# A sum of two tiles made by an adding transfer in place of GpSimd's tensor_tensor

## The chip, the cores and the metric

The kernel runs on one core of one Trainium2 chip. The core has five engines, each with its own instruction stream: TensorE (PE; its weight loads are listed apart as PEld), VectorE (DVE), ScalarE (ACT), GpSimd (POOL) and SyncE (SP). They meet only at semaphores. Sixteen DMA engines move data between the chip's memory (HBM) and the on-chip SBUF, and within SBUF. PSUM is the memory that PE writes its products to. The metric is the device time of one execution in microseconds (us); lower is better.

## What is computed

Two parts, cut to what matters. The first is a causal convolution over the sequence with a softmax of seven taps for each of eight heads. The second, on its output x, is two products with a rational function between them:

```
w = softmax(weight)                     # 8 heads x 7 taps
x[s] = sum over k of w[k] * x_padded[s + k]
h = x @ w_in                            # 32768 x 192, 192 x 2048
P = a0 + a1*h + a2*h^2 + a3*h^3
Q = 1 + |b0|*|h| + |b1|*h^2
out = (P / (Q + 1e-6)) @ w_out          # 2048 x 192
```

Everything is float32 on the outside; there are 32768 tokens.

## The kernel before

The tokens are taken in 64 chunks of 512. For each chunk PE makes the convolution (steps c, as small matmuls with a band of taps), then the first product in eight units of 2 x 128 rows of h (steps g1; a unit is a tile of 128 x 1024 float32 in PSUM, named hp), and, one chunk later, the second product (steps g2, tile op) from the eight results g. Between the products stand the elementwise steps of a unit, named by letters:

- hs (ACT, L334): copies h from PSUM to SBUF. p (POOL, L340) and u (POOL, L347) begin the cubic from that copy: t = (-a3*hs - a2)*hs. In unit 3 ACT (L328) and VectorE begin it from PSUM; in units 4 and 7 ACT (L328) does p.
- v (DVE, L351): goes on with the cubic, and is the last reader of h.
- A (ACT, L354): |b0 h|. B (ACT, L357): |b1| h^2.
- Q (POOL, L360): A + B, written over A.
- L (ACT, L363): the logarithm of A + B + 1 + 1e-6, written over B. Y (ACT, L366): exp(-L), the reciprocal, tile y in PSUM, of which there is one.
- m (DVE, L370): the cubic times y. e (DVE, L375): y times the denominator, which it reads from A. g (DVE, L379): a Newton step that refines the quotient; its tile g feeds PE.

So in one unit Q waits for A and B, L waits for Q, Y for L, m for Y, and e reads A as well.

The order of the steps on PE, ACT, DVE and POOL is written out by hand: START is the first two rounds, with the conversion of the weights from float64 among them (steps wi and wo; `L227`, `L233`, `L237`, `L245` on DVE, `L241` on POOL), PLAN is one round of the steady part, used 61 times, and END is the rest. Each engine takes its steps strictly in that order, so a step that waits holds up all that is behind it on its engine. The steps on which the prediction rests stand so in PLAN (after the point: how many chunks late):

```
c0a.0 L7.2 m6.2 u1.1 g12a.1 O1.2 A1.1 e6.2 g12b.1 B1.1 Q0.1 g6.2 g20a.1 hs2.1 c0b.0 v1.1 g20b.1 Y7.2
c0c.0 p2.1 L0.1 ...
```

SBUF tiles come from pools: t, A, B have four buffers each, hs three, g eleven. DMAs are issued by SyncE: the inputs, two loads of x per chunk (xs) and two stores of results per chunk (out). GpSimd issues none.

Of the kernel before, what the change touches and what calls it, by code (L numbers as in the profile page):

```python
# [16 lines left out]
ALU = mybir.AluOpType  # L17
# [20 lines left out]
F64_MIN = float(np.uint32(0x38000000).view(np.float32))  # L38


# The order in which the engines take the steps of one chunk of tokens: step, unit or half,
# piece; after the point, how many chunks later than the first step of its chunk it is taken.
PLAN = """
c0a.0 L7.2 m6.2 u1.1 g12a.1 O1.2 A1.1 e6.2 g12b.1 B1.1 Q0.1 g6.2 g20a.1 hs2.1 c0b.0 v1.1 g20b.1 Y7.2
c0c.0 p2.1 L0.1 m7.2 g13a.1 B2.1 u2.1 g13b.1 e7.2 A2.1 g20c.1 g7.2 A3.1 g20d.1 Q1.1 g21a.1 v2.1 Y0.1
# [6 lines left out]
g11a.0 m5.1 p0.0 B0.0 g11b.0 e5.1 u0.0 L6.1 g27a.1 g5.1 hs1.0 g27b.1 g27c.1 p1.0 v0.0 Y6.1 g27d.1  # L52
"""

# How a unit's cubic begins. H: on VectorE, from PSUM; U: on GpSimd; V: on ScalarE, then GpSimd.
MODES = "UUUHVUUV"

# The first two rounds, with the preparation of the weights (wi: w_in, wo: w_out; step, piece);
# after the point the chunk.
START = """  # L60
wia0.0 c0a.0 wim0.0 wis0.0 c1a.0 wid0.0 wia1.0 c1b.0 wio0.0 wim1.0 wir0.0 c1c.0 wis1.0 c0b.0 c0c.0
xh1.0 wid1.0 wia2.0 wih0.0 xl1.0 wio1.0 xh0.0 wir1.0 wim2.0 wid2.0 wia3.0 wil0.0 wia4.0 xl0.0 wis2.0
# [13 lines left out]
L6.0 e5.0 u0.1 wor7.0 hs1.1 g5.0 p1.1 Y6.0 v0.1 wor4.0  # L76
"""

# What remains after the last full round; after the point the chunks from the end.
END = """  # L80
u1.2 L7.3 m6.3 B1.2 O1.3 c0a.1 g12a.2 A1.2 g12b.2 Q0.2 e6.3 hs2.2 c0b.1 g6.3 Y7.3 g20a.2 v1.2 A2.2
B2.2 c0c.1 g20b.2 m7.3 g20c.2 p2.2 g20d.2 g21a.2 e7.3 g13a.2 g13b.2 g21b.2 g7.3 g21c.2 u2.2 xh0.1
# [26 lines left out]
def kernel(  # L109
# [12 lines left out]
    nc = tc.nc  # L122
# [13 lines left out]

    nc.scalar.preload_act_table_set("natural_log_exp_and_others")

# [1 line left out]
    wb_t = const.tile([P, NG, BW], F32, name="wb_t")  # L140
    mb_t = const.tile([P, NG, BW], F32, name="mb_t")
    wr_t = const.tile([P, NG, KT], F32, name="wr_t")
# [15 lines left out]
        nc.sync.dma_start(out=t[0:BLK, 0:3 * XF // 4], in_=xa[c])  # L158
        nc.sync.dma_start(out=t[BLK:, 3 * XF // 4:], in_=xb[c])

# [1 line left out]
    mx = const.tile([P, NG], F32, name="mx")  # L162
    sm = const.tile([P, NG], F32, name="sm")
    nc.vector.tensor_reduce(out=mx, in_=wr_t, axis=AX.X, op=ALU.max)
# [7 lines left out]
    nc.vector.tensor_tensor(out=wb_t, in0=wb_t, in1=mb_t, op=ALU.mult)  # L172
    nc.vector.tensor_tensor(out=wb_t, in0=wb_t, in1=sm[:, :, None].broadcast_to([P, NG, BW]), op=ALU.mult)

# [1 line left out]
    cf = const.tile([P, 6], F32, name="cf")  # L176
    nc.vector.tensor_scalar(cf[:, 0:4], ab_t[:, 0:4], -1.0, None, ALU.mult)
    nc.scalar.activation(out=cf[:, 4:6], in_=ab_t[:, 4:6], func=AF.Abs)
# [15 lines left out]
        scales.append(reg)  # L194
    r_be0, r_sq1, r_a3 = scales

# [1 line left out]
    # In integers: the upper word's digits, rebiased, then the lower word's, rounded, added.  # L198
    wh_t = const.tile([P, UPC, 2, 2, P], F32R, name="wh_t")
    wl_t = const.tile([P, UPC, 2, 2, P], F32R, name="wl_t")  # L200
    wo_t = const.tile([P, FT, D], F32, name="wo_t")
# [43 lines left out]
            nc.vector.tensor_tensor(out=wl_t[:, i].rearrange("p a b c -> p (a b c)"), in0=w["t"],  # L245
                                    in1=wh_t[:, i].rearrange("p a b c -> p (a b c)").bitcast(F32), op=ALU.subtract)

# [1 line left out]
    def stat(c, blk, g):  # L249
        t = xs_buf[c % 2].rearrange("p (m b g) -> p m b g", m=32, b=NBLK)  # L250
        return t[:, :, blk, g]
# [24 lines left out]
            xh = X[c, "B"]  # L276
            nc.vector.tensor_tensor(out=xh[64:P], in0=cps[0:64], in1=xh[0:64].bitcast(F32), op=ALU.subtract)

# [1 line left out]
    H = {}  # L280

    def gemm1(k, j):
# [5 lines left out]
        for n, (w, part, x) in enumerate(terms):  # L288
            nc.tensor.matmul(H[k][:, j, :], lhsT=w[:, i, part, j, :], rhs=x, start=(n == 0), stop=(n == len(terms) - 1))  # L289

# [1 line left out]
    G = {}  # L292
    O = {}

# [18 lines left out]
        nc.scalar.copy(out=ob, in_=O.pop((c, pair))[:, :, 0:D])  # L313
        nc.sync.dma_start(out=out_v[c, pair], in_=ob)

# [1 line left out]
    st = {}  # L317

    def flat(k):
# [37 lines left out]
        nc.scalar.activation(out=tile_of(k, "B", work), in_=flat(k), func=AF.Square, scale=r_sq1)  # L357

    def step_Q(k):
        nc.gpsimd.tensor_tensor(out=st[k]["A"], in0=st[k]["A"], in1=st[k]["B"], op=ALU.add)  # L360

    def step_L(k):
        nc.scalar.activation(out=st[k]["B"], in_=st[k]["A"], func=AF.Ln, bias=C_Q)  # L363
# [13 lines left out]
    def step_g(k):  # L377
# [1 line left out]
        nc.vector.scalar_tensor_tensor(out=g, in0=st[k]["y"], scalar=2.0, in1=g, op0=ALU.subtract, op1=ALU.mult)  # L379
        del st[k], H[k]  # L380

# [1 line left out]
    unit_steps = {"hs": step_hs, "p": step_p, "u": step_u, "v": step_v, "A": step_A, "B": step_B, "Q": step_Q,  # L383
                  "L": step_L, "Y": step_Y, "m": step_m, "e": step_e, "g": step_g}
    CP = {}
# [27 lines left out]
            else:  # L413
                unit_steps[kind](c * UPC + n)

# [1 line left out]
    def steps(text):  # L417
        return [(kind, int(n), "abcd".find(piece) if piece else 0, int(c))
                for kind, n, piece, c in re.findall(r"(g1|g2|w[io][a-z]|[A-Za-z]+)(\d)([a-d]?)\.(\d+)", text)]

    order = steps(START)
# [67 lines left out]
```

## Time and profile before

| | |
|---|---|
| median of 3 runs | 2808.53 us (2807.76 to 2809.02) |
| span of the profiled execution, first to last instruction | 2807.8 us |
| time of an execution beside that span | the three runs stand 0.0 to 1.2 us over the span; the median 0.7 us |
| busy share of the span | PE 98%, PEld 88%, DVE 96%, ACT 96%, POOL 96% |
| granted clock of PE, mean | 0.991 of full |
| DMA | 61.22 MB on SyncE's queue, 7.9% of 16 engines |

The profile is one execution, taken by the hardware profiler. Its page lists busy times, the chain of work that ended last, groups of instructions (line, engine, operation, tiles written <- read, shapes, count | busy us, mean ns of one | idle us just before them and what ended it), and DMA issues (size, median us from issue to landing). Other views of the same trace used here: the stages (a row for each stretch of time, with each engine's busy us and number of instructions), the waits (engine and line that waited, for whom, total us, times, longest), and the order of time (start us, duration us, instruction, and in brackets the idle time before it). A busy PE is not proof of PE at its peak, and idle time of an engine that does not set the pace costs nothing.

### The profile page before, as it was taken

What the parts mean: (1) busy time and instruction counts of PE and PEld (TensorE: products, weight loads), DVE (VectorE), ACT (ScalarE), POOL (GpSimd) and SP (SyncE); (2) the same over time, 40 slices, a digit from 0 to 9 for tenths busy, and PEclk for the clock granted to TensorE, in tenths of its full rate; (3) what the DMA queues carried; (4) which work ended last, traced back from release to release, by engine and by line L of the source; (5) the groups of instructions that cost most, each with busy time, mean ns of one, the idle gap of its engine ahead of it and who ended that gap; (6) DMA issues with size and microseconds to landing.
All of it is one profiled execution on the core that took longest, in us unless ns stands there. A gap on an engine that the chain in (4) does not pass through costs nothing.

```text
span 2807.8 us, 50193 instructions
## 1 busy us (share of the span) xinstructions
PE 2748.3 (98%) x20224; PEld 2458.2 (88%) x20224; DVE 2683.3 (96%) x2309; ACT 2688.4 (96%) x2990; POOL 2684.4 (96%) x1304
## 2 busy tenths in 40 slices
PE   4799999999999999999999999999999999999999
PEld 3688988988889889889889888888898898898888
DVE  8999999999999999999999999999999999999998
ACT  6899999999999999999999999999999999999997
POOL 6899999999999999999999999999999999999996
PEclk8899999999999999999999999999999999999999
DMA  4000000000000000000000000000000000000000
GB/s 136 10 16 25 22 16 25 22 16 25 21 17 22 19 22 22 19 22 22 16 25 22 16 25 22 16 22 19 22 22 19 22 22 16 25 22 16 25 9 15
DMA packets 49193, 64.43 MB, mean 23 GB/s; under 512 B 4672, under 2 KB 43840, under 8 KB 48960
## 3 DMA queue, kind: packets, MB, share of 16 engines
q1 hardware_dynamic: 48960, 61.22, 7.9%
q8 instruction: 159, 2.61, 0.4%
q14 instruction: 74, 0.61, 0.1%
HBM read 36.03 MB, written 25.17 MB: 22 GB/s over the span
## 4 chain that ended last, share of the span: by engine, by line
PE 96%; DVE 2%; issue 1%; ACT 0%; DMA 0%; SPq 0%; ACTq 0%; DVEq 0%
PE op L306 48%; PE hp L289 42%; PE cps L259 6%; DVE ad L227 0%; PE cps L306 0%; DVE t L351 0%; DVE wl_t L245 0%; DMA g<-in_w_in 0%; DVE g L370 0%; DVE y L375 0%; DVE tr L233 0%; DVE tr L237 0%; DVE wo_t L233 0%; DVE g L379 0%; DVE wo_t L237 0%
## 5 line engine op out<-in xcount | busy, mean ns | idle before, releaser
L306 PE MATMUL op<-wo_t,g 128*128 128x192 f32 x8128 | 1420.8, 326 | 0.0
L306 PEld LDWEIGHTS op<-wo_t,g 128*128 128x128 f32 x8128 | 1344.6, 189 | 43.9
L360 POOL TENSOR_TENSOR A<-A,B 128x1024 f32<-128x1024 f32 x512 | 1219.2, 2388 | 28.4 <-ACT B L357 26.1
L347 POOL TENSOR_TENSOR t<-t,hs 128x1024 f32<-128x1024 f32 x448 | 1077.9, 2406 | 48.6 <-ACT hs L334 16.3
L289 PE MATMUL hp<-xh,wh_t 128*128 128x512 f32 x2048 | 872.9, 426 | 45.9 <-DVE t L351 41.4
L370 DVE SCALAR_TENSOR_TENSOR g<-t,cf,y 128x1024 f32<-128x1024 f32 x512 | 654.4, 1278 | 57.0 <-ACT y L366 46.6
L351 DVE SCALAR_TENSOR_TENSOR t<-t,cf,hp 128x1024 f32<-128x1024 f32 x512 | 652.5, 1274 | 32.7 <-POOL t L347 29.9
L379 DVE SCALAR_TENSOR_TENSOR g<-y,g 128x1024 f32<-128x1024 f32 x512 | 626.9, 1224 | 17.5
L289 PE MATMUL hp<-xh,wl_t 128*128 128x512 f32 x2048 | 637.7, 393 | 0.0
L375 DVE SCALAR_TENSOR_TENSOR y<-A,y 128x1024 f32<-128x1024 f32 x512 | 625.5, 1222 | 0.0
L363 ACT ACTIVATE B<-A 128x1024 f32<-128x1024 f32 x512 | 547.0, 1069 | 0.2 <-POOL A L360 0.2
L366 ACT ACTIVATE y<-B 128x1024 f32<-128x1024 f32 x512 | 528.8, 1033 | 15.6 <-DVE g L379 14.6
L354 ACT ACTIVATE A<-hp 128x1024 f32<-128x1024 f32 x512 | 528.0, 1031 | 15.8 <-PE hp L289 15.7
L357 ACT ACTIVATE B<-hp 128x1024 f32<-128x1024 f32 x512 | 528.7, 1033 | 0.0
L289 PEld LDWEIGHTS hp<-xh,wh_t 128*128 128x128 f32 x2048 | 388.8, 190 | 124.4 <-DVE t L351 32.6
L334 ACT COPY hs<-hp 128x1024 f32<-128x1024 f32 x448 | 457.2, 1020 | 35.4 <-PE hp L289 34.1
L289 PEld LDWEIGHTS hp<-xh,wl_t 128*128 128x128 f32 x2048 | 388.2, 190 | 87.5
L289 PE MATMUL hp<-xl,wh_t 128*128 128x512 f32 x1024 | 405.5, 396 | 2.4 <-DVE xl L273 2.4
L340 POOL TENSOR_SCALAR t<-hs,cf 128x1024 f32<-128x1024 f32 x320 | 389.6, 1217 | 10.8 <-ACT hs L334 3.9
L328 ACT ACTIVATE t<-hp,cf 128x1024 f32<-128x1024 f32 x192 | 214.7, 1118 | 25.3 <-PE hp L289 22.8
L259 PEld LDWEIGHTS cps<-wb_t,xs 128*32 128x32 f32 x6876 | 162.5, 149 | 65.8 <-issue 64.3
L289 PEld LDWEIGHTS hp<-xl,wh_t 128*128 128x128 f32 x1024 | 195.4, 191 | 23.7 <-DVE xl L273 2.9
(49 smaller groups left out, 632.6 us busy)
## 6 DMA issues: line engine op xcount, KB each, us to landing
out<-ob SPq DMA_DIRECT2D x128, 192.0 KB, 2.0
xs<-in_xa SPq DMA_DIRECT2D x64, 324.0 KB, 3.9
xs<-in_xb SPq DMA_DIRECT2D x64, 108.0 KB, 3.7
g<-in_w_in SPq DMA_DIRECT2D x8, 512.0 KB, 9.4
g<-in_w_out SPq DMA_DIRECT2D x8, 384.0 KB, 9.3
wb_t<-in_wband SPq DMA_DIRECT2D x1, 174.0 KB, 2.4
mb_t<-in_mband SPq DMA_DIRECT2D x1, 174.0 KB, 2.4
wr_t<-in_wrep SPq DMA_DIRECT2D x1, 21.0 KB, 1.9
```

Of the source, the lines that this page charges most:

```text
L289: nc.tensor.matmul(H[k][:, j, :], lhsT=w[:, i, part, j, :], rhs=x, start=(n == 0), stop=(n == len(terms) - 1))
L306: nc.tensor.matmul(op[:, t, 0:D], lhsT=g[:, f % 2, tok:tok + P], rhs=wo_t[:, f, :], start=(f == 0 and t == 0), stop=(f == FT - 1 and t == 1))
L347: nc.gpsimd.tensor_tensor(out=t, in0=t, in1=st[k]["hs"], op=ALU.mult)
L351: nc.vector.scalar_tensor_tensor(out=t, in0=t, scalar=a1, in1=flat(k), op0=ALU.add, op1=ALU.mult)
L354: nc.scalar.activation(out=tile_of(k, "A", work), in_=flat(k), func=AF.Abs, scale=r_be0)
L357: nc.scalar.activation(out=tile_of(k, "B", work), in_=flat(k), func=AF.Square, scale=r_sq1)
L360: nc.gpsimd.tensor_tensor(out=st[k]["A"], in0=st[k]["A"], in1=st[k]["B"], op=ALU.add)
L363: nc.scalar.activation(out=st[k]["B"], in_=st[k]["A"], func=AF.Ln, bias=C_Q)
L366: nc.scalar.activation(out=tile_of(k, "y", ps_y), in_=st[k]["B"], func=AF.Exp, scale=-1.0)
L370: nc.vector.scalar_tensor_tensor(out=G[k].rearrange("p a b -> p (a b)"), in0=st[k]["t"], scalar=a0, in1=st[k]["y"], op0=ALU.add, op1=ALU.mult)
L375: nc.vector.scalar_tensor_tensor(out=y, in0=st[k]["A"], scalar=C_Q, in1=y, op0=ALU.add, op1=ALU.mult)
L379: nc.vector.scalar_tensor_tensor(out=g, in0=st[k]["y"], scalar=2.0, in1=g, op0=ALU.subtract, op1=ALU.mult)
```

## The change

The step Q is no longer an instruction of GpSimd that adds, but a transfer from SBUF to SBUF, issued by GpSimd at the same place in its order, which reads B and adds it to A where A lies. Comments of the file were blanked out as well, without moving a line.

```diff
     def step_Q(k):
-        nc.gpsimd.tensor_tensor(out=st[k]["A"], in0=st[k]["A"], in1=st[k]["B"], op=ALU.add)
+        nc.gpsimd.dma_start(out=st[k]["A"], in_=st[k]["B"], accum_op=ALU.add)
```

No step changes its place. On GpSimd, in the steady part, from Q of unit 7 to the three Q's that follow each other (units 1, 3, 2); before:

```order
L360 TENSOR_TENSOR A<-A,B 128x1024
L340 TENSOR_SCALAR t<-hs,cf 128x1024
L347 TENSOR_TENSOR t<-t,hs 128x1024
L340 TENSOR_SCALAR t<-hs,cf 128x1024
L347 TENSOR_TENSOR t<-t,hs 128x1024
L360 TENSOR_TENSOR A<-A,B 128x1024
L340 TENSOR_SCALAR t<-hs,cf 128x1024
L347 TENSOR_TENSOR t<-t,hs 128x1024
L360 TENSOR_TENSOR A<-A,B 128x1024 x3
```

and after (p and u of units 0 and 1 stand between the first two Q's, of units 7 and 0; p and u of unit 2 behind them):

```order
L360 DMA A<-B 128x1024
L340 TENSOR_SCALAR t<-hs,cf 128x1024
L347 TENSOR_TENSOR t<-t,hs 128x1024
L340 TENSOR_SCALAR t<-hs,cf 128x1024
L347 TENSOR_TENSOR t<-t,hs 128x1024
L360 DMA A<-B 128x1024
L340 TENSOR_SCALAR t<-hs,cf 128x1024
L347 TENSOR_TENSOR t<-t,hs 128x1024
L360 DMA A<-B 128x1024 x3
```

Only the kind of instruction is another. On ScalarE the order is the same too, but the semaphores differ. Around L of unit 7 (the first L363 here) and of unit 0 (the second), with what each instruction waits for, before:

```order
L363 ACTIVATE B<-A 128x1024 [waits Pool_49]
L313 COPY ob<-op 128x384 [waits DMAHW3_49,PE_49]
L354 ACTIVATE A<-hp 128x1024
L357 ACTIVATE B<-hp 128x1024
L334 COPY hs<-hp 128x1024 [waits PE_49]
L366 ACTIVATE y<-B 128x1024 [waits DVE_49,Activation_49]
L363 ACTIVATE B<-A 128x1024 [waits Pool_49]
```

and after:

```order
L363 ACTIVATE B<-A 128x1024 [waits DMASW7_49]
L313 COPY ob<-op 128x384 [waits DMAHW3_49,PE_49]
L354 ACTIVATE A<-hp 128x1024
L357 ACTIVATE B<-hp 128x1024
L334 COPY hs<-hp 128x1024 [waits PE_49,Pool_49]
L366 ACTIVATE y<-B 128x1024 [waits DVE_49,Activation_49]
L363 ACTIVATE B<-A 128x1024 [waits DMASW0_49]
```

L now waits for the transfer's landing (DMASW, one of eight semaphores in turn) and no longer for GpSimd's addition; the copy hs has a wait for GpSimd of its own, for a buffer that u has read, which L's wait covered before.

## The prediction, written before the result

> **What bounds the kernel now.** I read the page's busy times and chain first, then the table by stage, then who waits in the middle of the run, and last the order of time on ScalarE (ACT) and GpSimd (POOL) around one Q step. Page, then the stages (us, then busy us of PE, PEld, DVE, ACT and POOL with instructions, granted clock, DMA share, GB/s):
>
> ```profile
> PE 2748.3 (98%) x20224; PEld 2458.2 (88%) x20224; DVE 2683.3 (96%) x2309; ACT 2688.4 (96%) x2990; POOL 2684.4 (96%) x1304
> PE 96%; DVE 2%; issue 1%; ACT 0%; DMA 0%; SPq 0%; ACTq 0%; DVEq 0%
> ```
>
> ```profile
> 0.00:70.00 70.00, 31.71 (x283) 24.07 (x284) 61.70 (x71) 45.66 (x67) 48.36 (x33) 0.83 0.45 136
> 70.00:140.00 70.00, 52.45 (x328) 44.09 (x327) 67.66 (x63) 59.35 (x70) 62.65 (x33) 0.83 0.04 10
> 700.00:2100.00 1400.00, 1400.00 (x10362) 1254.62 (x10362) 1346.47 (x1149) 1364.94 (x1510) 1361.85 (x656) 1.00 0.08 21
> ```
>
> PE is busy in all 1400 us of the middle at the full clock, and the chain runs through PE: nothing that GpSimd gives up can shorten a round there. All of PE's idle time that could be had back lies in the first 140 us (38.3 + 17.6 us) and a few us at the end. But the others are close behind. A round (one chunk of tokens, eight units) takes 42.67 us, by the chain in order of time, where the same matmuls come back (start us, us):
>
> ```profile
> 1395.04 3.90 PE op L306 x24
> 1437.71 3.90 PE op L306 x24
> ```
>
> The 1400 us hold 32.8 rounds. Idle per round is then (1400 - 1364.94) / 32.8 = 1.07 us on ScalarE, 1.63 us on VectorE, 1.16 us on GpSimd. Who waits there (total us, times, longest):
>
> ```profile
> DVE g L370 <- ACT y L366: 21.1, 66, 0.5
> DVE t L351 <- POOL t L347: 15.5, 65, 0.4
> ACT hs L334 <- PE hp L289: 13.7, 33, 0.4
> ```
>
> No L step (L363, the logarithm) waits for Q, and PE waits for nobody. So the question is not what GpSimd saves but whether Q's result still comes in time for L, on a ScalarE that can lose 1.07 us in a round and no more.
>
> **What is taken off GpSimd.** From the page:
>
> ```profile
> L360 POOL TENSOR_TENSOR A<-A,B 128x1024 f32<-128x1024 f32 x512 | 1219.2, 2388 | 28.4 <-ACT B L357 26.1
> L347 POOL TENSOR_TENSOR t<-t,hs 128x1024 f32<-128x1024 f32 x448 | 1077.9, 2406 | 48.6 <-ACT hs L334 16.3
> ```
>
> 512 additions of 2.39 us, 1219 us, go; what it takes to issue a transfer comes in their place. Per round 8 x 2.38 = 19.0 us of 41.5 go, so an issue may cost up to 2.39 + 1.16 / 8 = 2.5 us before GpSimd becomes the bound. Worth in the middle: nothing, since PE has no wait to give back. VectorE's waits for u (15.5 us) become fewer, which PE doesn't feel.
>
> **What is added: Q becomes a transfer that ScalarE waits for.** Every transfer has 128 rows of 4 KB, 0.52 MB; B is read, A is read, A is written. What matters is the time from Q's turn on GpSimd to the semaphore on which L waits. I call it the landing, with the issue in it. What is allowed is read at unit 0, where Q and L stand closest. ScalarE (start us, us):
>
> ```profile
> 1377.58 1.02 ACT L357 ACTIVATE B<-hp 128x1024 f32<-128x1024 f32 x1
> 1379.57 1.01 ACT L334 COPY hs<-hp 128x1024 f32<-128x1024 f32 x1
> 1380.56 1.03 ACT L366 ACTIVATE y<-B 128x1024 f32<-128x1024 f32 x1
> 1381.52 1.04 ACT L363 ACTIVATE B<-A 128x1024 f32<-128x1024 f32 x1
> 1382.47 0.46 ACT L313 COPY ob<-op 128x384 f32<-128x384 f32 x1
> 1382.83 1.03 ACT L354 ACTIVATE A<-hp 128x1024 f32<-128x1024 f32 x1
> 1383.75 1.02 ACT L357 ACTIVATE B<-hp 128x1024 f32<-128x1024 f32 x1
> 1385.19 1.02 ACT L334 COPY hs<-hp 128x1024 f32<-128x1024 f32 x1 [0.42 <-PE hp L289]
> 1386.10 1.03 ACT L366 ACTIVATE y<-B 128x1024 f32<-128x1024 f32 x1
> 1387.06 1.05 ACT L363 ACTIVATE B<-A 128x1024 f32<-128x1024 f32 x1
> ```
>
> GpSimd beside it:
>
> ```profile
> 1380.69 1.20 POOL L340 TENSOR_SCALAR t<-hs,cf 128x1024 f32<-128x1024 f32 x1
> 1381.97 2.42 POOL L347 TENSOR_TENSOR t<-t,hs 128x1024 f32<-128x1024 f32 x1
> 1384.34 2.40 POOL L360 TENSOR_TENSOR A<-A,B 128x1024 f32<-128x1024 f32 x1
> ```
>
> B of unit 0 is ready at 1378.6 (first row), yet Q starts at 1384.34: in GpSimd's order it stands behind p and u of unit 1, and p begins when hs of unit 1 ends (1379.57 + 1.01). A less loaded GpSimd doesn't help: hs, p and u keep their times, so Q's turn stays where it is. L of unit 0 is the last row of ScalarE, at 1387.06. The gap is 2.72 us, just more than the 2.40 us of the addition. Behind a late L stand B and A of unit 2, A of unit 3, Y of unit 0 and all the rest of ScalarE; m on VectorE waits for that Y, and already waits for a Y twice in a round; POOL's next Q waits for a B behind it. Since hs, p, u and Q are all counted from a step of ScalarE ahead of L, the gap moves with ScalarE and the stall comes back every round. ScalarE takes up 1.07 us. So **a landing over 2.72 + 1.07 = 3.79 us makes every round longer by what it is over**, in each of the 61 rounds of the table PLAN.
>
> The others have more room: unit 1's Q began at 1390.36 and its L at 1393.97 (3.61 us, and its L is moved back by unit 0's stall while its Q isn't); unit 7 has 6.96 us, unit 2 7.07 us less one issue:
>
> ```profile
> 1390.36 2.38 POOL L360 TENSOR_TENSOR A<-A,B 128x1024 f32<-128x1024 f32 x1
> 1393.17 2.40 POOL L360 TENSOR_TENSOR A<-A,B 128x1024 f32<-128x1024 f32 x1 [0.43 <-ACT B L357]
> 1417.23 2.38 POOL L360 TENSOR_TENSOR A<-A,B 128x1024 f32<-128x1024 f32 x1
> ```
>
> ```profile
> 1393.97 1.07 ACT L363 ACTIVATE B<-A 128x1024 f32<-128x1024 f32 x1
> 1400.24 1.09 ACT L363 ACTIVATE B<-A 128x1024 f32<-128x1024 f32 x1
> 1424.19 1.05 ACT L363 ACTIVATE B<-A 128x1024 f32<-128x1024 f32 x1
> ```
>
> (The second Q row is unit 3's; unit 2's Q is next behind it, and the second L row is unit 2's.)
>
> **How long is a landing?** No accumulating transfer and none issued by GpSimd stands in this trace. The nearest rows are SyncE's transfers (median us to landing) and the queue in the window from 11 to 18 us, when it was full of the weights' long rows:
>
> ```profile
> out<-ob SPq DMA_DIRECT2D x128, 192.0 KB, 2.0
> wr_t<-in_wrep SPq DMA_DIRECT2D x1, 21.0 KB, 1.9
> q1 hardware_dynamic: 48960, 61.22, 7.9%
> ```
>
> ```profile
> DMA packets 724, 2.68 MB, mean 382 GB/s; under 512 B 81, under 2 KB 85, under 8 KB 723
> ```
>
> One pass over 0.524 MB at 382 GB/s is 1.37 us. Low end: the 192 KB row and the missing 0.33 MB at that rate, 2.0 + 0.86 = 2.9 us, one pass and no cost of issuing. High end: three passes one after the other (two read, one written) at the whole run's rate, 61.22 MB in 7.9% of 2807.8 us or 276 GB/s, 1.90 us each; the 1.9 us of a transfer with hardly any data; and an issue as dear as the addition, 2.39 us: 10.0 us. I take two passes, since an engine must read two operands for each result and can write while it reads, at the rate of long rows, plus 1.9 us, plus 0.1 us for an issue whose price I don't know: 2.74 + 1.9 + 0.1 = 4.7 us. It is nearest to the low end because the 4 KB rows are like the weights' rows, and the queue is free: 8 x 2.74 = 22 us in a round of 42.67, on top of a share of 8%.
>
> The Trainium skill (DMA: Bandwidth & Descriptors, section Anatomy of one DMA) fits a GpSimd transfer as 2.0 us plus bytes over 436 GB/s; that would be an estimate of 3.2 us here, under the limit, and no change at all. The skill's Collectives: The Full Stack (section The bandwidth ceiling) says that an add inside the DMA engine costs no time of its own but needs two source reads on one ring, which halves the rate; no run here shows either, and the sum above goes by the rows.
>
> Middle: 61 x (4.7 - 3.79) = 61 x 0.91 = +55.5 us.
>
> **The start.** Sixteen of the additions lie in the first 140 us, where VectorE paces and is held up by GpSimd:
>
> ```profile
> L227 DVE TENSOR_SCALAR ad<-ad 128x512 f32<-128x512 f32 (+1 forms) x16 | 12.2, 766 | 4.1 <-ACT ad L223 4.1
> 90.44 2.55 DVE L227 TENSOR_SCALAR ad<-ad 128x384 f32<-128x384 f32 x1
> 90.42 2.35 POOL L360 TENSOR_TENSOR A<-A,B 128x1024 f32<-128x1024 f32 x1
> 74.97 0.35 DVE L227 TENSOR_SCALAR ad<-ad 128x384 f32<-128x384 f32 x1
> ```
>
> The same instruction takes 0.35 us free and 2.55 us when an addition began just before it and ended with it. In the order of time VectorE is held up by an addition at five places, by 8.7 us in all; the row shown is the last of them and lost 2.2 us. Other GpSimd work moves up into the place and holds VectorE up instead, and the first chunk's L can come late, so of -9 to +5 I take -3 us. At the end of the run the last Y waits 2.0 us for VectorE ahead of its turn, which covers a landing 2 us longer than the addition: 0.
>
> **Sum.** 2807.8 (span) + 0.7 (to the median, 2808.5) + 55.5 - 3 = 2861 us.
>
> **Rivals.**
> First, no change: a landing of at most 3.8 us, 0.9 us less than I take. For it: the low end, 2.9 us, and the skill's fit. Against it: two reads. PE then keeps its 42.67 us: 2808.5 less the 3 of the start, 2806.
> Second, a landing of 6 to 10 us (a slow adder, or a dear issue on GpSimd). At 7 us unit 0 alone gives 61 x (7 - 3.79) = +196 us: 3004 us. From 7 us on units 2 and 7 stall as well and each further us counts about twice; at 10 us 61 x (6.2 + 3) = +561, 3370 us. An issue over 2.5 us makes GpSimd the bound: at 3.5 us 61 x 8 x 1.0 = +490.
> Third, faster: the landing stays under 3.8 us and VectorE gets the whole 8.7 us of the start back, of which PE, waiting for VectorE there, keeps all: 2800 us. It decides from 5.6 us on.
>
> **Chances.** Of this kernel a measurement can tell about 0.2%, 5.6 us. Forecast (landing 3.8 to 6 us): 0.52, its own range 2806 to 2943 (61 x 2.21 = 135 above). Second rival: 0.24. No change: 0.17. Faster: 0.07. Slower by over 0.2% is 0.52 + 0.24 less a little for landings just over the limit: 0.74; within 0.2%: 0.19; faster: 0.07. The range leaves out the faster case and the slowest 0.12, landings over some 7.5 us: 2803 to 3050.
>
> **What the changed profile would show.** Right: L363 on ScalarE waits for a DMA, once in a round and about 2 us long; GpSimd's busy share falls to about 60% or less; PE gets idle time in the middle, waiting for ScalarE or VectorE, and a round takes about 43.6 us. Wrong: rounds of 42.67 us with L's wait under 1.1 us (the first rival); waits of L at units 2 and 7 too, or GpSimd busy over 95% (the second). My forecast hangs on the landing alone: each us moves the time by 61 us.

## The result: 109 us slower

| | before | after |
|---|---|---|
| median of 4 runs | 2808.62 us (2807.76 to 2809.02) | 2917.84 us (2913.57 to 2918.72) |
| ratio to before, 95% | | 1.0387 [1.0372, 1.0402] |
| profiled execution, its span | 2808.5, 2807.8 us | 2913.57, 2911.8 us |
| steady round, mean of 40 | 42.68 us | 44.50 us |

The forecast was 2861 us, 52 us slower. The direction and the place were right, the size was half of what was measured. The profiled execution of after is the shortest of its four; 104 us of the 109 can be followed in its trace. One run of the kernel with unit 0 alone (10303 us) and one of the kernel with all transfers early (11115 us), kernels that follow below, had a granted clock of about a quarter and are left out of the medians.

### The profile page after: what moved, and what is told of

Its sections match the earlier page's. It is cut to its first block, busy times and chain, and to the rows that moved or that the text cites. A ratio compares the mean times of both kernels' runs of the same rounds, so it can differ in the third digit from the quotient of the medians.

```text
span 2911.8 us, 50960 instructions
## 1 busy us (share of the span) xinstructions
PE 2790.6 (96%) x20224; PEld 2456.6 (84%) x20224; DVE 2669.0 (92%) x2309; ACT 2678.9 (92%) x2990; POOL 1920.0 (66%) x1304
## 3 DMA queue, kind: packets, MB, share of 16 engines
q0 software_dynamic: 73728, 268.47, 48.9%
## 4 chain that ended last, share of the span: by engine, by line
ACT 41%; DMA 22%; POOL 12%; issue 12%; PE 10%; DVE 4%; SPq 0%; ACTq 0%; POOLq 0%; DVEq 0%
DMA A<-B 22%; ACT A L354 8%; ACT B L357 8%; ACT y L366 8%; ACT hs L334 8%; POOL t L347 6%; ACT B L363 6%; PE hp L289 5%; POOL t L340 5%; PE op L306 4%; ACT t L328 2%; ACT xh L267 1%; DVE y L375 1%; DVE t L351 1%; POOL A L360 1%
## 5 line engine op out<-in xcount | busy, mean ns | idle before, releaser
L363 ACT ACTIVATE B<-A 128x1024 f32<-128x1024 f32 x512 | 545.9, 1067 | 165.6 <-DMA A<-B 165.5
L360 POOL DMA_DIRECT2D A<-B x512 | 448.4, 915 | 339.6 <-ACT B L357 315.4
L366 ACT ACTIVATE y<-B 128x1024 f32<-128x1024 f32 x512 | 529.8, 1035 | 6.1 <-DVE g L379 5.7
L354 ACT ACTIVATE A<-hp 128x1024 f32<-128x1024 f32 x512 | 519.7, 1028 | 0.0
L334 ACT COPY hs<-hp 128x1024 f32<-128x1024 f32 x448 | 454.1, 1014 | 37.5 <-PE hp L289 34.1
L328 ACT ACTIVATE t<-hp,cf 128x1024 f32<-128x1024 f32 x192 | 217.1, 1131 | 2.3 <-PE hp L289 2.3
```

Of the source, the lines that this page charges most:

```text
L334: nc.scalar.copy(out=tile_of(k, "hs", hpool), in_=flat(k))
L354: nc.scalar.activation(out=tile_of(k, "A", work), in_=flat(k), func=AF.Abs, scale=r_be0)
L366: nc.scalar.activation(out=tile_of(k, "y", ps_y), in_=st[k]["B"], func=AF.Exp, scale=-1.0)
```

## The profile after

The page: busy times, the chain that ended last, the transfers' queue and issues, and the two groups of the change:

```profile
PE 2790.6 (96%) x20224; PEld 2456.6 (84%) x20224; DVE 2669.0 (92%) x2309; ACT 2678.9 (92%) x2990; POOL 1920.0 (66%) x1304
q0 software_dynamic: 73728, 268.47, 48.9%
ACT 41%; DMA 22%; POOL 12%; issue 12%; PE 10%; DVE 4%; SPq 0%; ACTq 0%; POOLq 0%; DVEq 0%
L363 ACT ACTIVATE B<-A 128x1024 f32<-128x1024 f32 x512 | 545.9, 1067 | 165.6 <-DMA A<-B 165.5
L360 POOL DMA_DIRECT2D A<-B x512 | 448.4, 915 | 339.6 <-ACT B L357 315.4
A<-B POOLq DMA_DIRECT2D x512, 512.0 KB, 4.6
```

The chain was 96% PE; now it is a loop of ScalarE, GpSimd and the transfer, and PE carries 10% of it. GpSimd got 764 us of time back, and nobody gained by it: the logarithm L363 waits 165.5 us for the transfer. The stages (us; then busy us of PE, PEld, DVE, ACT, POOL with instructions; granted clock, DMA share, GB/s):

```profile
0.00:70.00 70.00, 34.64 (x286) 25.70 (x286) 60.36 (x81) 49.96 (x73) 42.22 (x36) 0.83 0.67 179
70.00:140.00 70.00, 59.91 (x377) 50.33 (x378) 62.53 (x59) 61.20 (x70) 47.98 (x33) 0.88 0.45 88
700.00:2100.00 1400.00, 1362.39 (x9966) 1201.67 (x9965) 1290.99 (x1102) 1304.23 (x1448) 933.11 (x631) 1.00 0.57 114
```

In the middle PE is idle for 37.6 us where it had no idle time, at the same granted clock, and every engine does 4% fewer instructions (PE 9966 for 10362). In the first 140 us it is the other way: PE does 663 instructions for 611. Who waits in the middle (total us, times, longest; four rows of the view; GpSimd's waits for ScalarE are longer):

```profile
ACT B L363 <- DMA A<-B: 78.8, 62, 3.1
DVE t L351 <- ACT A L354: 44.2, 31, 2.4
PE hp L289 <- DVE t L351: 35.1, 62, 1.9
ACT hs L334 <- PE hp L289: 14.5, 32, 0.5
```

The three upper rows were not there before, and each hands its wait to the next: L waits for the transfer, VectorE for the A that stands behind L on ScalarE, PE for VectorE to free hp. 62 waits in 31.5 rounds are two per round. The lower row was there before and is as long as it was. One round on ScalarE, in order of time:

```profile
1428.33 1.02 ACT L357 ACTIVATE B<-hp 128x1024 f32<-128x1024 f32 x1
1429.81 1.02 ACT L334 COPY hs<-hp 128x1024 f32<-128x1024 f32 x1 [0.46 <-PE hp L289]
1430.72 1.03 ACT L366 ACTIVATE y<-B 128x1024 f32<-128x1024 f32 x1
1434.16 1.06 ACT L363 ACTIVATE B<-A 128x1024 f32<-128x1024 f32 x1 [2.40 <-DMA A<-B]
...
1447.27 1.06 ACT L363 ACTIVATE B<-A 128x1024 f32<-128x1024 f32 x1 [0.28 <-DMA A<-B]
```

GpSimd beside it, at Q of unit 0 and at Q of units 3 and 2:

```profile
1428.93 0.89 POOL L360 DMA_DIRECT2D A<-B  x1
...
1440.12 1.75 POOL L360 DMA_DIRECT2D A<-B  x2 [4.70 <-ACT B L357]
```

And the same two transfers in the chain:

```profile
1428.93 5.20 DMA A<-B
...
1440.66 6.59 DMA A<-B
```

The large wait is unit 0's: Q at 1428.93, L at 1434.16. The small one is unit 2's, which the forecast had at nothing: its transfer stands second in the queue behind unit 3's. Over 40 rounds, worked out from the order of time, unit 0's landing (Q's turn to L's start) is 4.62 to 5.96 us, median 4.85, mean 4.93. ScalarE's idle time in a round, before and after, in us:

| | before | after |
|---|---|---|
| L of unit 0, for the transfer | 0 | 2.12 |
| L of unit 2, for the transfer | 0 | 0.41 |
| hs of unit 2 (L334), for PE | 0.41 | 0.45 |
| t of unit 7 (L328), for PE | 0.33 | 0 |
| A of unit 3 (L354), for PE | 0.26 | 0 |
| sum | 1.00 | 2.98 |

The two waits that are gone in after were in before:

```profile
ACT t L328 <- PE hp L289: 10.8, 33, 0.3
ACT A L354 <- PE hp L289: 8.5, 33, 0.3
```

## The experiments

The theory: the whole loss is L's wait at unit 0 and, less, at unit 2, on a ScalarE whose own idle time makes up for little of it. The first rival: the traffic. Eight transfers of 0.5 MB in a round, which hold the 16 DMA engines for 48.9% of the span, slow the loads, the stores and each other, and undoing one wait would not help. The second rival: the wait would be cheap, but something that is not on ScalarE (GpSimd's issues, VectorE) lengthens the round.

**One unit alone, and all but that one.** The transfer for unit 0 only (64 of 512), the addition elsewhere; and the reverse.

```diff
     def step_Q(k):
-        nc.gpsimd.dma_start(out=st[k]["A"], in_=st[k]["B"], accum_op=ALU.add)
+        if k % UPC == 0:        # the second kernel: != 0
+            nc.gpsimd.dma_start(out=st[k]["A"], in_=st[k]["B"], accum_op=ALU.add)
+        else:
+            nc.gpsimd.tensor_tensor(out=st[k]["A"], in0=st[k]["A"], in1=st[k]["B"], op=ALU.add)
```

> Only unit 0's sum is a transfer (64 of 512); the other seven are GpSimd's tensor_tensor again. Theory: nearly the whole loss stays: unit 0's L waits about 2.0 us, a round is 42.67 + 2.0 - 0.6 = 44.1 us, 61 x 1.4 = +86, 2893 us (2880 to 2905). Rival (traffic): an eighth of the loss, 2808.6 + 109 / 8 = 2822 us.

> Unit 0's sum is GpSimd's tensor_tensor, the other seven are transfers (448 of 512). Theory: no L waits long; unit 2's 0.3 to 0.4 us fits into ScalarE's idle time; 42.67 us a round and 2802 to 2809 us. Rival (traffic): seven eighths of the loss, 2904 us.

Unit 0 alone: 2900.3 us, ratio 1.0329 [1.0309, 1.035], round 44.21. Its queue on the page, and who waits in the middle (three added lines make L363 L366 here):

```profile
q0 software_dynamic: 9216, 33.56, 6.2%
```

```profile
ACT B L366 <- DMA A<-B: 65.6, 32, 3.3
```

An eighth of the transfers, which hold the engines for 6.2% of the span, keeps 92 of the 109 us. That speaks against the traffic: the loss follows the place and not the amount. The forecast's own term for unit 0, 61 x 0.91, would have given 2864 here, so the fault lies in that term. The other 448 transfers gave 2837.26 us, 1.0103 [1.0087, 1.012], where 2802 to 2809 was expected. The reason for the miss:

```profile
ACT B L366 <- DMA A<-B: 35.4, 36, 1.5
```

One wait a round again, but of unit 1, 0.96 us in the mean, in a round of 43.22 us. Unit 1 had 3.61 us between Q and L, less than a landing. In after its L came late enough by unit 0's wait that this did not show. A stall hid the next one.

**Q of unit 0 half a step earlier.** By the rows of before, B of unit 0 is ready 5.7 us ahead of Q's turn (1378.60, 1384.34), so Q can stand in the table ahead of p and u of unit 1:

```diff
 PLAN
-c0a.0 L7.2 m6.2 u1.1 g12a.1 O1.2 A1.1 e6.2 g12b.1 B1.1 Q0.1 g6.2 ...
+c0a.0 L7.2 m6.2 u1.1 g12a.1 O1.2 A1.1 e6.2 g12b.1 B1.1 g6.2 ...
-g11a.0 m5.1 p0.0 B0.0 g11b.0 e5.1 u0.0 L6.1 ...
+g11a.0 m5.1 p0.0 B0.0 g11b.0 e5.1 u0.0 Q0.0 L6.1 ...
 START
-L6.0 e5.0 u0.1 wor7.0 ...
+L6.0 e5.0 u0.1 Q0.1 wor7.0 ...
 END
-... g12a.2 A1.2 g12b.2 Q0.2 e6.3 ...
+... g12a.2 A1.2 g12b.2 e6.3 ...
```

> Q of unit 0 stands ahead of p and u of unit 1 in GpSimd's order, in every round; all 512 transfers stay. Theory (landing): the loss is the time that unit 0's L waits for a landing of 4.9 us in a gap of 2.8 us. Q0 then begins some 4 us earlier, L of unit 0 waits no more, unit 2's wait of 0.3 to 0.4 us stays and fits into ScalarE's idle time; a round takes 42.67 us and the time is 2802 us (2808.6 less the 6.6 us that the start gained), 2798 to 2812. Rival (traffic): 512 transfers that hold 49% of the DMA engines slow the chip whatever the order; the time stays at 2905 to 2918.

2812.46 us, 1.0015 [1.0005, 1.0024], round 42.84. Moving one instruction takes 105 of the 109 us back, with all 512 transfers in place. The 10 us above the expectation are unit 1 again, and the end of the run:

```profile
ACT B L363 <- DMA A<-B: 20.5, 37, 1.4
```

**Unit 2's transfer ahead of unit 3's.** Q of unit 2 moved to stand next to Q of unit 1, one row up in the table.

```diff
-c0c.0 p2.1 ... g20d.1 Q1.1 g21a.1 v2.1 Y0.1
-g21b.1 B3.1 ... p4.1 g21d.1 Q2.1 g22a.1 u3.1 Y1.1
+c0c.0 p2.1 ... g20d.1 Q1.1 Q2.1 g21a.1 v2.1 Y0.1
+g21b.1 B3.1 ... p4.1 g21d.1 g22a.1 u3.1 Y1.1
```

> Only in the steady rounds Q of unit 2 goes ahead of Q of unit 3, so that it no longer stands behind it in the DMA queue. Theory: unit 2's wait of 0.41 us a round is a second term, added in full: 61 x 0.41 = 25 us less, 2893 us (2885 to 2900), and L of unit 2 waits no more. Rival: that wait lies in time that unit 0's wait has already cost, and 2918 us stay (2912 to 2920).

2904.51 us, 1.0339 [1.0322, 1.0356], round 44.38. Who waits in the middle:

```profile
ACT B L363 <- DMA A<-B: 69.8, 32, 3.2
ACT t L328 <- PE hp L289: 9.3, 32, 0.9
PE hp L289 <- DVE t L351: 36.5, 62, 1.9
```

32 waits for 62: unit 2's is gone, all of its 0.41 us. The round fell by only 0.12, because t's wait for PE (0.27 us) came back. On its own unit 2's wait was worth a third of its length: the time lies between the theory's range and the rival's, and neither was right.

**All transfers early enough.** Both moves, and Q of unit 1 at the place that Q of unit 0 had, right behind B of unit 1; all 512 additions still by transfer.

```diff
-... g12b.1 B1.1 Q0.1 g6.2 ...    # all else as in the two kernels above
+... g12b.1 B1.1 Q1.1 g6.2 ...
-... g20d.1 Q1.1 g21a.1 v2.1 Y0.1
+... g20d.1 Q2.1 g21a.1 v2.1 Y0.1
```

> GpSimd's order is changed for three transfers of every steady round: unit 0's Q ahead of p and u of unit 1, unit 1's ahead of p and u of unit 2, unit 2's ahead of unit 3's. All 512 sums are transfers. Theory (landing in too short a gap): every L then has at least 6.9 us after its Q's turn, more than the 4.9 us of a landing; no L waits, PE has no idle time, a round takes 42.68 us, and the 8 to 10 us that the start gained are left: 2799 us (2796 to 2803). Rival (something of the drift of 0.16 us a round with unit 0 alone moved, which is left, comes from the 49% share of the DMA engines): 2808 to 2812 us.

2804.84 us, 0.9989 [0.998, 0.9999]. Its queue on the page, and the only waits of ScalarE in the middle:

```profile
q0 software_dynamic: 73728, 268.47, 50.8%
```

```profile
ACT hs L334 <- PE hp L289: 15.7, 32, 0.5
ACT t L328 <- PE hp L289: 9.3, 33, 0.3
ACT A L354 <- PE hp L289: 6.5, 32, 0.2
```

The rounds are back at 42.69 us with the same bytes in the same number of packets, and ScalarE waits for PE at its three old places and for no transfer. So where L comes late enough the traffic and the issues cost the steady part nothing, and as the cause of the loss both rivals fall. (To the landing the traffic may add a little: unit 0's took 4.61 us by the median where it was the only transfer, and 4.85 with all eight.) The 6 us above the expectation lie in the end of the run (below).

**How much of a wait does ScalarE take up?** Three kernels in the order with unit 2's transfer first, each with a transfer that should take less time.

```diff
-        nc.gpsimd.dma_start(out=st[k]["A"], in_=st[k]["B"], accum_op=ALU.add)
+        nc.gpsimd.dma_start(out=st[k]["A"][:, 0:768], in_=st[k]["B"][:, 0:768], accum_op=ALU.add)   # first
+        nc.gpsimd.dma_start(out=st[k]["A"][:, 0:512], in_=st[k]["B"][:, 0:512], accum_op=ALU.add)   # second
+        nc.gpsimd.dma_start(out=st[k]["A"], in_=st[k]["B"])                                         # third
```

> As the kernel with unit 2's Q ahead of unit 3's (2904.5 us, a round of 44.38), but the transfer adds 768 of the 1024 columns; the other quarter is left unadded. Theory: two passes of 128 KB less at 382 GB/s shorten the landing by 0.69 us, unit 0's wait falls from 2.14 to 1.45 us, and of a wait ScalarE takes up 0.44 us: 61 x (1.45 - 0.44) = +62 less 8 for the start, 2862 us (2855 to 2870). The prediction's rule (1.07 us taken up): 61 x 0.38 = +23 less 8, 2824 us. Rival (the landing doesn't depend on the size): 2904.

> The same with 512 of the 1024 columns; the other half is left unadded. Theory: the landing is 1.38 us shorter, unit 0's wait 0.76 us, a round 42.68 + 0.76 - 0.44 = 43.0 us: +20 less 8, 2820 us (2810 to 2828). The prediction's rule (1.07 us taken up): no longer rounds, 2800 us.

> The same order with all 1024 columns, but the transfer only copies B over A and adds nothing. Theory (the second read is what the adding costs the engines): a packet of 4 KB takes half of the 348 ns that it takes now, the landing is 1.4 us shorter, as with half the columns, and the time is 2820 us (2810 to 2828). Rival (the issue and the semaphore, not the second read): the landing stays over 4.5 us and the time over 2890 us.

| transfer | time, ratio [95%] | landing of unit 0 | L's wait in a round | round over 42.68 | taken up |
|---|---|---|---|---|---|
| 1024 columns added | 2904.51, 1.0339 [1.0322, 1.0356] | 4.85 | 2.14 | 1.70 | 0.44 |
| 768 added | 2854.65, 1.0164 [1.0149, 1.018] | 4.18 | 1.41 | 0.93 | 0.48 |
| 512 added | 2811.78, 1.0012 [1.0003, 1.0022] | 3.55 | 0.74 | 0.27 | 0.47 |
| 1024 copied | 2803.79, 0.9984 [0.9974, 0.9993] | 3.09 | 0.39 | 0.12 | 0.27 |

(us; landings are medians, waits and rounds are means, over 40 rounds.) The middle of the run for the 768 columns, for the 512, and for the copy, each from its own waits:

```profile
ACT B L363 <- DMA A<-B: 45.7, 32, 2.6
```

```profile
ACT B L363 <- DMA A<-B: 23.5, 32, 1.5
```

```profile
ACT B L363 <- DMA A<-B: 11.6, 32, 2.5
```

All three came out below their expectations, by 7, 8 and 16 us, the first and the third below their ranges; their starts are 11 to 13 us ahead of that of before, more than was expected. The column on the right settles the size: of three waits between 0.74 and 2.14 us ScalarE takes up 0.44 to 0.48, not 1.07. The 0.27 of the copy is a mean of two kinds of round. Taken one by one in the order of time, 35 of its 40 rounds have a wait of 0.17 to 0.41 us, and they are as long as without it (one is 0.09 us longer); the other five have 0.59 to 2.49 us, and each is longer by that less 0.46 to 0.49. So the reserve is about 0.47 us in every round: a wait within it is free, and all beyond it is paid. Two stretches of the copy's trace, L of unit 0 in three rounds that follow each other (start us, us):

```profile
736.67 1.06 ACT L363 ACTIVATE B<-A 128x1024 f32<-128x1024 f32 x1 [0.38 <-DMA A<-B]
780.29 1.06 ACT L363 ACTIVATE B<-A 128x1024 f32<-128x1024 f32 x1 [1.33 <-DMA A<-B]
822.88 1.06 ACT L363 ACTIVATE B<-A 128x1024 f32<-128x1024 f32 x1 [0.38 <-DMA A<-B]
```

```profile
1038.07 1.06 ACT L363 ACTIVATE B<-A 128x1024 f32<-128x1024 f32 x1 [0.18 <-DMA A<-B]
1080.98 1.06 ACT L363 ACTIVATE B<-A 128x1024 f32<-128x1024 f32 x1 [0.41 <-DMA A<-B]
1123.42 1.06 ACT L363 ACTIVATE B<-A 128x1024 f32<-128x1024 f32 x1 [0.18 <-DMA A<-B]
```

From first to last the upper three take 86.21 us, 0.86 over two rounds of 42.68 (1.33 less 0.47); the lower three take 85.35, so the wait of 0.41 cost nothing.

By the forecast's rule, 3.79 us allowed, the 768 columns would have lost 61 x 0.39 = 24 us and the 512 nothing; the rounds lost 0.93 and 0.27 us, 57 and 16 us in 61. The copy moves as many bytes as the full addition and loses next to nothing (it holds the engines half as long, see the end): it is not the bytes that count but the landing.

**The start and the end by themselves.** In the order given: the transfer in the first two chunks only, in the order of after; then, in the order with all transfers early, the addition back in the last two chunks; and the addition back in the first two.

```diff
     def step_Q(k):
-        nc.gpsimd.dma_start(out=st[k]["A"], in_=st[k]["B"], accum_op=ALU.add)
+        if k < 2 * UPC:      # first kernel; second: k < 62 * UPC; third: k >= 2 * UPC
+            nc.gpsimd.dma_start(out=st[k]["A"], in_=st[k]["B"], accum_op=ALU.add)
+        else:
+            nc.gpsimd.tensor_tensor(out=st[k]["A"], in0=st[k]["A"], in1=st[k]["B"], op=ALU.add)
```

> Only the first two chunks' sums (16 of 512) are transfers; all else is the kernel before, its order too. Theory: the start's gain comes from these 16 alone, since GpSimd's additions no longer hold up VectorE's preparation of the weights: 6 to 10 us less, 2800 us (2798 to 2803). Rival (the start gains because GpSimd is less loaded later on as well): within 2 us of 2808.

> As the kernel with all three Q's early (2804.8 us), but the last two chunks' sums (16 of 512) are GpSimd's tensor_tensor again. Theory: the 6 us that are lost after the last full round are six waits of L for a landing, and they go: 2798 us (2796 to 2801), faster than both kernels. Rival (they come from another order of GpSimd's steps there): 2805.

> As the kernel with all three Q's early, but the first two chunks' sums are GpSimd's tensor_tensor, the other 496 transfers. Theory: no gain in the start, rounds of 42.68 us and 6 us lost at the end: 2814 us (2811 to 2817).

| transfer where | time, ratio [95%] | start (at chunk 2) | end (last result) |
|---|---|---|---|
| first two chunks only | 2801.79, 0.9977 [0.9968, 0.9986] | -7.8 | -8.0 |
| all, early | 2804.84, 0.9989 [0.998, 0.9999] | -10.7 | -4.0 |
| all but the last two chunks, early | 2799.48, 0.997 [0.9958, 0.9982] | -10.4 | -10.1 |
| all but the first two chunks, early | 2815.31, 1.0026 [1.0016, 1.0036] | +0.6 | +5.4 |

(us; the last two columns say how far ahead of before (-) or behind it (+) the same step stands in the order of time.) The three new kernels came out within their expected ranges. The terms are separate and nearly add up (-10.1 and +5.4 are -4.7, for -4.0 in the second row): the start is worth -8 to -11 us, the end +5 to +6, the middle nothing once the order gives the transfer its time. The third row is the fastest kernel of the study, faster than before and after. Its page reads like that of before, with GpSimd at 70%:

```profile
PE 2751.0 (98%) x20224; PEld 2459.6 (88%) x20224; DVE 2665.9 (95%) x2309; ACT 2683.9 (96%) x2990; POOL 1944.8 (70%) x1304
PE 96%; DMA 1%; POOL 1%; ACT 1%; issue 0%; DVE 0%; SPq 0%; POOLq 0%; ACTq 0%
```

## Why the forecast had the right cause and half the size

| step of the forecast | forecast | measured |
|---|---|---|
| landing at unit 0 | 4.7 us | 4.85 |
| L's wait there, in a round | 4.7 - 2.72 = 1.98 | 2.12 |
| **what ScalarE takes up** | **1.07** | **0.44 to 0.48** |
| what unit 2 adds | 0 | 0.12 |
| a round | +0.91 | +1.83 |
| 61 rounds | +55.5 | +106.0 |
| start | -3 | -6.6 |
| end | 0 | +4.5 |
| span | +52.5 | +104 |

(us. +106 is the lag gained from chunk 2 to chunk 63 in the trace of after, 1.74 us a round; the 40 in the middle, of which the other numbers are means, run at 1.83. What the median has above this, 109.2 against 104, is within the 5 us by which the runs of after differ, and no trace shows it.)

**The landing** was right, by errors that cancel. The two passes were 2.74 us in the forecast, and each transfer holds the engines for 48.9% x 2911.8 / 512 = 2.78 us. The issue was put at 0.1 us and takes 0.89; the rest, put at 1.9 us, is 4.85 - 2.78 - 0.89 = 1.2. The Trainium skill (DMA: Bandwidth & Descriptors, Anatomy of one DMA) gives 3.2 us by its fit, an estimate; the trace agrees for a copy (3.09 us) and not for a transfer that adds.

**L's wait, its place and its return in every round** were right: once a round, unit 0, 2.12 us. (The mean landing is 4.93 us, and the gap, landing less wait, is 2.82 in this trace, 0.1 us more than in before.)

**"ScalarE takes up 1.07 us" is the step that failed.** It took all of the mean idle time per round for a reserve. But idle time on an engine that works in order helps a late step only where it lies behind that step and is not already part of the gap. The forecast's own rows show that a part of it was: the addition began at 1384.34, and the copy hs with its 0.42 us of idle time began after that, at 1385.19, before L at 1387.06. Those 0.42 us are inside the 2.72 that the transfer was allowed, and were counted again in the 1.07. What lies behind L is 0.33 + 0.26 = 0.59 us, t of unit 7 and A of unit 3. Nor is all of that free, since the late L makes PE late too, through A, VectorE and hp. In the kernel with unit 2 first, which takes up 0.44, A's wait is gone, t's is still there with 0.27 and that of hs is 0.49: the three fell from 1.00 to 0.76. The other 0.20 is the net of delays shorter than the 0.15 us from which the view lists a wait, the two largest of them: in before A of unit 3, its listed wait taken off, follows A of unit 2 after 1.03 us and t of unit 4 follows L of unit 1 after 1.07; here it is 0.90 and 0.95. The reserve is the largest part of what the forecast fell short by in a round, some 0.6 of 0.92 us; L's longer wait is 0.14 and unit 2 is 0.12. With 0.45 in place of 1.07 the forecast's own sum is 61 x 1.53 = +93 us, and with the landing that was measured 61 x 1.67 = +102.

**Unit 2** was given 7.07 us less one issue, and a landing of 4.7. Its transfer stands behind unit 3's, which holds the engines for 2.78 us, so it lands 6.6 us after its issue. The forecast subtracted the issue of the transfer ahead and not its time on the engines.

**Unit 1** (3.61 us) was seen as short, with its L moved back by unit 0's stall. That was right for after, where its L never waits, and it is what came up when unit 0 was mended.

**GpSimd** was to be busy 60% or less; it is 66%, since an issue costs 0.9 us and not 0.1. It waits for ScalarE instead (339.6 us ahead of Q), so as GpSimd's load this cost nothing; as a part of the landing it is counted above.

**The start** had the right mechanism. (What is prepared there are the two weight matrices, which come in as float64, so not everything is float32 on the outside.) The same group as before, first 140 us of after, with the conversion of wo beside it, and then the waits of PE and of L there:

```profile
L227 DVE TENSOR_SCALAR ad<-ad 128x512 f32<-128x512 f32 (+1 forms) x16 | 6.7, 425 | 3.9 <-ACT ad L223 3.9
L233 DVE TENSOR_SCALAR wo_t<-ad 128x384 uint32<-128x384 uint32 x8 | 4.2, 531 | 0.0
```

```profile
PE hp L289 <- DVE t L351: 31.8, 10, 6.8
ACT B L363 <- DMA A<-B: 9.6, 4, 3.6
```

In before the second of these groups and PE's wait were:

```profile
L233 DVE TENSOR_SCALAR wo_t<-ad 128x384 uint32<-128x384 uint32 x8 | 9.5, 1204 | 0.0
```

```profile
PE hp L289 <- DVE t L351: 41.4, 9, 7.7
```

L227 went from 12.2 to 6.7 us, this part of L233 from 9.5 to 4.2, PE's wait from 41.4 to 31.8. In these two groups VectorE got 10.8 us back, more than the 8.7 us that were counted at five places, and the forecast kept only 3 of them for fear of late L's. Four L's are late in the first 140 us, by 9.6 us in all, and the net is -6.6 with them; with Q of unit 0 earlier it is -10.7. So the start lay inside its -9 to +5, at twice the -3 that was taken.

**The end** was covered by one wait of Y, by the forecast. In the last 74 us of the kernel with all transfers early L waits six times:

```profile
ACT B L363 <- DMA A<-B: 6.0, 6, 1.7
```

The forecast looked at the last unit only; here L waits at six units.

**The rivals.** No change (0.17) and faster (0.07) needed a landing under 3.8 us; it was 4.85. A landing of 6 us or more (0.24) did not come for unit 0. One sign that was named for it, a wait at unit 2, did come, but from the place in the queue; L of unit 7 never waits in the middle. With the right reserve the limit is 2.72 + 0.45 = 3.17 us, or 3.3 with the gap of 2.82; the copy, at 3.09, stayed under it in 35 of 40 rounds.

## What to carry to other kernels

Before an engine's idle time is counted as a reserve for a late step, find where in the round it lies: what stands between the releasing instruction and the late step is part of the gap already, and only what stands behind it can make up for the delay. Between a producer and a consumer a transfer needs latency, which an order by hand must give it, and a queue adds the engine time of each transfer that is ahead. Here one moved instruction was worth 105 us, while 764 us less work on an engine that did not set the pace were worth nothing in the steady part; and a removed stall should be followed by a look at the next smallest gap.

## What the runs showed of the hardware

- A transfer from SBUF to SBUF that adds, 128 rows of 4 KB, holds the 16 engines for 2.78 us; a copy of the same tile for 24.2% x 2803.4 / 512 = 1.33 us:

```profile
q0 software_dynamic: 73728, 268.47, 24.2%
```

The number of packets and bytes on the page is the same, so the bytes do not show the second read. The Trainium skill (Collectives: The Full Stack, The bandwidth ceiling) gives an add two source reads and half the rate; the ratio here, 2.1, agrees.
- The landing is the engines' time and about 2.0 us, whatever the size: 4.85 - 2.78, 4.18 - 2.17 (39.0% x 2852.7 / 512) and 3.55 - 1.54 (28.0% x 2810.8 / 512) for 1024, 768 and 512 columns; 3.09 - 1.33 = 1.8 for the copy, whose issue is 0.3 us shorter. These are unit 0's landings; the full transfers of units 6 and 7 land 4.5 us after their issue in after, and why unit 0's take 0.3 us longer is not shown.
- The issue takes GpSimd 0.89 us for a transfer that adds and 0.60 us for a copy.
- Half of the DMA engines' time in use (50.8%) did not lengthen a steady round: 42.69 us for 42.68.
